# End of a segment in layer A: order of the last values, scores and output rounds, and a second home for an attention output

## The chip, the cores and the metric

The kernel runs on one core of a Trainium2 chip. Its metric is the device time of one execution in microseconds (us), as the median of several runs. Engines: TensorE (PE in the profile, its weight loads PEld), VectorE (DVE), ScalarE (ACT), GpSimd (POOL) and SyncE (SP). Each engine works through its own queue in order and waits for the others by semaphores. DMA transfers are issued here from SP's queue (weights) and from POOL's queue (small rows).

## The reference, cut to what matters

Four layers, A B A B, each added to the residual. Layer A, the one that the change touches, walks through the 2048 tokens in 64 segments of 32 tokens. Eight memory rows come ahead of each segment; they are the first eight output rows of the segment before, so segments can't be computed side by side.

```
for s in range(n_seg):                       # 64 segments
    h = concat([mem, x[32 s : 32 s + 32]])   # 40 rows of 640
    q, k, v = h @ Wq, h @ Wk, h @ Wv         # 32 heads of 192
    p = softmax(mask(q k^T * scale))         # 40 x 40 per head
    o = (p v) @ Wo                           # 40 rows of 640
    mem = o[:8]; out = o[8:]
```

Layer B is a linear attention with a learned feature map over all tokens. It is not changed.

## The kernel before, in words

`layer_A` first runs `A_pre`, which computes K, Q and V of the last eight tokens of every segment for all segments at once and stores them in DRAM (`kqb`, `vb`). `A_chain` then walks through the 64 segments, and this serial walk is most of the kernel's time. All bf16 weights of a layer A don't fit on the chip with the rest, so part of Wq, Wk and Wv goes through slots that SP loads again in every segment (`load_slot`, L661), and the twelve chunks of Wo for the first and last round share one region, `wo_end`, loaded again in every segment in six parts (`load_wo`, L678).

The 32 heads are worked in four rounds n = 0..3 of eight heads, in the order 0,1,2,3 in even segments and 3,2,1,0 in odd ones. For one round:

- `project` (L957) multiplies the transposed rows `hT` with the weights of one matrix: 5 steps of 4 matmuls, each into its own 32 rows of one PSUM bank (ps_qk for Q and K, ps_v for V). Where a piece of the weights lies in a slot, the matmul needs that slot's DMA.
- `to_raw` (ScalarE, L980) copies Q or K out of PSUM, `to_rows` (VectorE, L985) transposes it into QT or KT. `v_rows` (L994) copies V into one of two Vp tiles, one half on ScalarE, one on VectorE. KT has 80 columns for each of six row blocks: 64 from the transpose, 16 that POOL copies from kqb (`extra_kq`, L946). Rows 64 to 80 of Vp come by DMA from `vb` (`extra_v`, L953, the "V tail").
- `scores` (L1005): a matmul that writes the mask, then 6 with KT and QT, into ps_s. `weigh` (L1063) adds the exponential on ScalarE, giving E; for the last round E lies in the buffer of tag "raw".
- `sums` (L1079): a matmul with ones gives the softmax's sums. `normalise` (L1083): logarithm and exponential on ScalarE, a multiplication on VectorE (L1087).
- `attend` (L1018): 8 matmuls of Vp and E into two banks ps_o; ScalarE and VectorE copy one half each into OT (L1027, L1028). `keep_tail` and `store_tail` keep the 16 columns of the last eight tokens and store them by a POOL DMA. `tails_after` issues the V tail for two rounds later, and `next_kq` (L1071) copies the next round's extra keys and queries and loads the `kqb` after next.
- `wo_round` (L1043): 12 steps of 4 matmuls that add OT times Wo into ps_w, one bank for the whole segment.

Nothing plans this order: `tc.manual_schedule()` leaves the instructions of every engine as they are written, and only the waits are put in. A round's parts are written one round apart, so that an attention, which needs finished weights E, stands behind the next round's projections. The loop `for n in range(L)` (L1133, L = 3) writes, for n = 0, 1, 2: Q of round n+1, attention n-1, scores n, K of round n+1, sums and normalisation n, output round n-1, V of round n+1 (not for n = 2). The end of the segment (from L1159) writes: scores 3, three fifths of V of round 3, attention 2, sums 3, the rest of V, output round 2, four filler matmuls (`keep_busy`, L1052, results unused), attention 3, five fillers, output round 3, five fillers, and `fill` (L1058), weight loads of one column. Then VectorE transposes the memory rows out of ps_w into the next `hT`, and the next segment's Q can begin. The attentions and rounds are named here by their place 0 to 3 in the segment; "second output round" in the change's title means the round with index 1.

Of the kernel before, what the change touches and what calls it, by code (L numbers as in the profile page):

```python
# [8 lines left out]
P = 128  # L9
BF16 = mybir.dt.bfloat16  # L10
# [8 lines left out]
LN_EPS = 1e-5  # L19

FILL = {0: 86, 2: 78}
SEG_FILL = 1

LATE = 64512
ARENA = 202752
# [90 lines left out]
class Kernel:  # L116
# [784 lines left out]
    def A_chain(self, xn_dram, at_dram, li, load_slot, piece, load_wo, late_wo, wo_mid, wo_end, low):  # L901
# [3 lines left out]
        with tc.tile_pool(name=f"A{li}_ch", reuse_waits="tile", bufs=1) as sp, \  # L905
# [3 lines left out]
            KT = sp.tile([P, 6, 80], BF16, name="KT")  # L909
# [105 lines left out]
                                         start=False, stop=(x == 1 and i == 2), skip_group_check=True)  # L1015
                return S

            def attend(E, n):  # L1018
                O = [pop.tile([P, 512], F32, name=f"ps_o{x}", tag=f"o{x}") for x in range(2)]
                for x in range(2):  # L1020
                    for k, e, i in ((0, 0, 0), (320, 1, 2), (128, 0, 1), (192, 1, 1)):
                        nc.tensor.matmul(O[x][:, 80 * i:80 * i + 80], lhsT=Vs[n % 2][0:80, 448 * x + k:448 * x + k + 128],  # L1022
                                         rhs=E[0:80, 160 * x + 80 * e:160 * x + 80 * e + 80], start=(k == 0),
                                         stop=(k == 192), skip_group_check=True)
                OT = sp.tile([P, 6, 64], BF16, name="OT", tag="OT")
                o = [x[:, 0:240].rearrange("p (i q) -> p i q", q=80) for x in O]
                nc.scalar.activation(out=OT[:, 0:3, :], in_=o[0][:, :, 0:64], func=ACT.Copy)  # L1027
                nc.vector.tensor_copy(out=OT[:, 3:6, :], in_=o[1][:, :, 0:64])  # L1028
                return OT, o

# [9 lines left out]
            def store_tail(otb, s, r):  # L1040
                nc.gpsimd.dma_start(out=self.otb_d[s, :, 96 * r:96 * r + 96], in_=otb[:, :, :].rearrange("p c t -> p (c t)"))  # L1041

            def wo_round(W, r, OT, first, last):  # L1043
                w = wo_end[:, :] if r in (0, 3) else wo_mid[:, 7680 * (r - 1):7680 * r]
                for i in range(12):
                    c, q = i % 6, 32 * (i // 6)
                    for g in range(4):
                        nc.tensor.matmul(W[32 * g:32 * g + 32, 0:160], lhsT=OT[:, c, q:q + 32],  # L1048
                                         rhs=w[:, 640 * i + 160 * g:640 * i + 160 * g + 160], start=(first and i == 0),
                                         stop=(last and i == 11), tile_position=(0, 32 * g), skip_group_check=True)  # L1050
# [51 lines left out]
            for s in range(NSEG):  # L1102
                W = pop.tile([P, 512], F32, name="ps_w", tag="w")
                order = rounds(s)
                L = NR - 1

                def q_or_k(m, n):
                    ps = pqp.tile([P, 512], F32, name="ps_qk", tag="qk")
                    project(hT, ps, m, n, s, range(KC))
                    return to_raw(ps, "OT" if m == "K" and n == 0 else "raw")  # L1110

                def v_banks():
                    return pop.tile([P, 512], F32, name="ps_v", tag="v")

                def tails_after(n):
                    if n + 2 < NR:
                        extra_v(s, n + 2)
                    elif s + 1 < NSEG:
                        extra_v(s + 1, n + 2 - NR)

                to_rows(q_or_k("Q", 0), "Q")
                if s == 0:
                    fill(FILL[li])
                to_rows(q_or_k("K", 0), "K")
                if s == 0:
                    late_wo(2)
                if s > 0:
                    store_rows(s - 1)
                pv = v_banks()
                project(hT, pv, "V", 0, s, range(KC))  # L1130
                v_rows(pv, 0)
                Ep = None
                for n in range(L):  # L1133
                    raw = q_or_k("Q", n + 1)
                    if n > 0:
                        OT, o = attend(Ep, n - 1)
                        tails_after(n - 1)
                    S, E = weigh(False)
                    to_rows(raw, "Q")
                    if n > 0:  # L1140
                        otb = keep_tail(o)
                    next_kq(s, n)
                    if n > 0:
                        store_tail(otb, s, order[n - 1])
                    to_rows(q_or_k("K", n + 1), "K")
                    sums(S, E)
                    normalise(S, E)
                    if n > 0:
                        wo_round(W, order[n - 1], OT, n == 1, False)
                        if n == 1:  # L1150
                            load_wo(order[L])
                            if s == NSEG - 1:
                                load_wo(3, low[:, 0:7680])
                    if n + 1 < L:
                        pv = v_banks()
                        project(hT, pv, "V", n + 1, s, range(KC))
                        v_rows(pv, n + 1)
                    Ep = E
                S, E = weigh(True)  # L1159
                pv = v_banks()  # L1160
                project(hT, pv, "V", L, s, range(3))
                OT, o = attend(Ep, L - 1)
                tails_after(L - 1)
                otb = keep_tail(o, True)
                next_kq(s, L)
                store_tail(otb, s, order[L - 1])
                sums(S, E)
                project(hT, pv, "V", L, s, range(3, KC))
                v_rows(pv, L, "x")
                normalise(S, E)  # L1170
                v_rows(pv, L, "a")
                if s + 1 < NSEG:
                    hT = new_hT()
                    hx_transpose(hT, range(1))
                wo_round(W, order[L - 1], OT, False, False)
                idle = pqp.tile([P, 512], F32, name="ps_idle", tag="qk")
                keep_busy(idle, 4, 192)
                OT, o = attend(E, L)
                tails_after(L)
                if s + 1 < NSEG:  # L1180
                    hx_transpose(hT, range(1, 4))
                    if s + 2 < NSEG:
                        load_rows(s + 2)
                keep_busy(idle, 5, 230)
                wo_round(W, order[L], OT, False, True)
                keep_busy(idle, 5, 230)
                fill(SEG_FILL)
                if s + 1 < NSEG:
                    wt = sp.tile([P, KC, 32], F32, name="wt", tag="raw")
                    for b0, b1 in ((2, 5), (0, 2)):  # L1190
                        nc.vector.transpose(out=wt[:, b0:b1, :], in_=W[:, 0:160].rearrange("p (j b) -> p b j", b=KC)[:, b0:b1, :])  # L1191
                        nc.vector.tensor_copy(out=hT[:, b0:b1, 0:8], in_=wt[:, b0:b1, 0:8])  # L1192
                store_tail(keep_tail(o), s, order[L])
                keep_rows(W)
# [73 lines left out]
```

## Time and profile before

| What | us |
|---|---|
| median of 3 runs (3625.7 to 3645.58) | 3634.94 |
| the profiled execution's own time | 3630.61 |
| its span, first to last instruction | 3628.6 |
| first layer A's chain, first to last counted segment | 206.5 to 1521.7 |
| second layer A's chain, likewise | 2027.0 to 3347.3 |

| Engine | busy us | share of the span |
|---|---|---|
| PE | 3489.8 | 96% |
| PEld | 2274.3 | 63% |
| DVE | 2329.9 | 64% |
| ACT | 2040.9 | 56% |
| POOL | 1591.3 | 44% |

How to read it: the shares are means over the whole kernel, and matmul ends are modelled, so a busy PE isn't a PE at its peak. The DMA engines moved 933.33 MB, a mean of 257 GB/s. A chain-of-waits line gives a start, a length and what ran. A row of the timeline gives start, length, engine, line, operation, names and shapes, and in brackets the idle time before it and what ended it. A row of the waits gives who waited for whom, the total in us, how often, and the longest. A row of DMA issues gives the KB of each and the median us from issue to landing.

### The profile page before, as it was taken

Reading aid. Unit: us, or ns where it says so; the run is one execution under the profiler, and the core shown is the slowest. Engines: PE = TensorE matmul, PEld = TensorE weight load, DVE = VectorE, ACT = ScalarE, POOL = GpSimd, SP = SyncE. Lnnn points to the kernel's source line nnn. Section 1 sums busy time; section 2 is a strip of 40 time slices with the busy share of each in tenths; the row PEclk is TensorE's granted clock in tenths of the full one; section 3 lists DMA queues with packets and bytes.
Section 4 is the critical chain, followed back from the end, with each engine's and each line's share of the span. In section 5 each row is a group of like instructions: output and inputs, shape, how many; then the busy total and the mean of one; then the engine's idle time right before and its main releaser. Section 6 shows DMA issues by size and latency. Waiting matters only on the chain.

```text
span 3628.6 us, 168597 instructions
## 1 busy us (share of the span) xinstructions
PE 3489.8 (96%) x70944; PEld 2274.3 (63%) x71270; DVE 2329.9 (64%) x6336; ACT 2040.9 (56%) x5233; POOL 1591.3 (44%) x4181
## 2 busy tenths in 40 slices
PE   9989999999999999989999899999999999999899
PEld 7756666666666666655377566666666666666553
DVE  5557666666666667646643566766666666667465
ACT  3356666666666666546432555666666666666463
POOL 3445555555555545430123454555545555555300
PEclk9999999999999999999999999999999999999999
DMA  8988887887888878860387877888888888888700
GB/s 295 339 292 292 283 290 277 292 293 276 290 294 282 281 279 296 289 202 1 138 271 203 304 271 268 292 288 286 279 292 284 280 283 288 295 275 291 230 1 30
DMA packets 533266, 933.33 MB, mean 257 GB/s; under 512 B 141066, under 2 KB 300442, under 8 KB 532506
## 3 DMA queue, kind: packets, MB, share of 16 engines
q1 hardware_dynamic: 431098, 821.50, 64.2%
q0 software_dynamic: 67744, 87.80, 8.3%
q10 hardware_dynamic: 33664, 13.24, 1.4%
q8 instruction: 557, 9.13, 1.0%
q14 instruction: 203, 1.66, 0.1%
HBM read 852.43 MB, written 73.73 MB: 255 GB/s over the span
## 4 chain that ended last, share of the span: by engine, by line
PE 68%; DMA 9%; DVE 8%; issue 6%; ACT 6%; PEld 2%; POOL 2%; SPq 0%; POOLq 0%; DVEq 0%; ACTq 0%
PE ps_qk L972 20%; PE ps_w L1048 8%; PE ps_v L972 8%; PE ps_o L1022 5%; PE ps_s L1014 4%; PE ps_pre L863 4%; DMA arena<-wo_rows 4%; DVE hT L928 3%; PE ps_s L1080 3%; PE ps_s L1009 2%; PE ps_pre L887 2%; PE ps_idle L1055 2%; DMA Vp<-vb 2%; ACT raw L982 2%; DVE E L1087 2%
## 5 line engine op out<-in xcount | busy, mean ns | idle before, releaser
L972 PEld LDWEIGHTS <-hT 128*32 128x32 bf16 x30720 | 738.8, 96 | 434.6 <-DVE hT L1192 29.5
L972 PE MATMUL ps_qk<-arena,hT 128*32 128x384 bf16 x20480 | 997.1, 327 | 13.1 <-DMA arena<-in_A_Wk_dram 3.1
L982 ACT ACTIVATE raw<-ps_qk 128x384 bf16<-128x384 f32 x1024 | 502.0, 490 | 381.1 <-PE ps_s L1080 245.7
L1048 PE MATMUL ps_w<-arena,OT 128*32 128x160 bf16 x24576 | 537.6, 235 | 25.9 <-issue 15.6
L955 POOL DMA_DIRECT2D Vp<-vb x512 | 258.3, 505 | 656.0 <-PE ps_o L1022 448.6
L972 PE MATMUL ps_v<-arena,hT 128*32 128x384 bf16 x10240 | 536.5, 329 | 6.0 <-DMA arena<-in_A_Wv_dram 6.0
L1048 PEld LDWEIGHTS <-OT 128*32 128x32 bf16 x24576 | 435.0, 97 | 114.7 <-issue 37.5
L987 DVE STREAM_TRANSPOSE KT<-raw 128x384 bf16<-128x384 bf16 x512 | 296.0, 578 | 196.5 <-ACT raw L982 192.5
L990 DVE STREAM_TRANSPOSE QT<-raw 128x256 bf16<-128x256 bf16 x512 | 227.9, 445 | 237.7 <-ACT raw L982 195.9
L943 POOL DMA_DIRECT2D kqb<-kqb x512 | 290.9, 568 | 173.6 <-POOL KT L951 147.6
L1003 DVE CAST Vp<-ps_v 64x384 bf16<-64x384 f32 x512 | 286.2, 559 | 95.7 <-ACT Vp L1001 80.8
L1001 ACT ACTIVATE Vp<-ps_v 64x384 bf16<-64x384 f32 x512 | 246.1, 481 | 151.0 <-PE ps_v L972 113.7
L1041 POOL DMA_DIRECT2D otb<-otb x512 | 282.8, 552 | 109.4 <-DVE otb L1037 94.5
L1028 DVE CAST OT<-ps_o 128x192 bf16<-128x192 f32 x512 | 182.9, 357 | 214.6 <-PE ps_o L1022 196.7
L1087 DVE TENSOR_TENSOR E<-E,ps_s 80x320 bf16<-80x320 bf16 x512 | 247.5, 483 | 73.6 <-ACT ps_s L1086 69.6
L1066 ACT ACTIVATE E<-ps_s 80x320 bf16<-80x320 f32 x512 | 221.4, 432 | 122.9 <-PE ps_s L1014 94.8
L1022 PEld LDWEIGHTS <-Vp 80*128 80x128 bf16 x4096 | 183.1, 99 | 160.3 <-issue 122.8
L1022 PE MATMUL ps_o<-E,Vp 80*128 80x80 bf16 x4096 | 234.0, 202 | 24.5 <-DMA Vp<-vb 4.5
L1014 PE MATMUL ps_s<-QT,KT 128*80 128x80 bf16 (+1 forms) x3072 | 233.2, 213 | 22.2 <-DVE KT L987 13.8
L1027 ACT ACTIVATE OT<-ps_o 128x192 bf16<-128x192 f32 x512 | 167.7, 328 | 147.7 <-PE ps_o L1022 147.7
L936 ACT ACTIVATE Vp<-ps_w 32x160 bf16<-32x160 f32 x512 | 150.3, 294 | 171.3 <-DVE wt L1191 146.1
L1014 PEld LDWEIGHTS <-KT 128*80 128x80 bf16 x3072 | 194.7, 119 | 70.6 <-issue 60.9
(151 smaller groups left out, 5213.8 us busy)
## 6 DMA issues: line engine op xcount, KB each, us to landing
arena<-wo_rows SPq DMA_DIRECT2D x792, 320.0 KB, 6.8
arena<-in_A_Wq_dram SPq DMA_DIRECT2D x427, 384.0 KB, 4.6
arena<-in_A_Wv_dram SPq DMA_DIRECT2D x427, 384.0 KB, 6.4
arena<-in_A_Wk_dram SPq DMA_DIRECT2D x768, 192.0 KB, 4.6
kqb<-kqb POOLq DMA_DIRECT2D x512, 48.0 KB, 5.1
arena<-in_A_Wk_dram SPq DMA_DIRECT2D x43, 384.0 KB, 7.0
vb<-arena POOLq DMA_DIRECT2D x128, 112.0 KB, 6.0
Vp<-vb POOLq DMA_DIRECT2D x512, 28.0 KB, 4.9
```

The source lines that it names most:

```text
L943: nc.gpsimd.dma_start(out=kqb[:], in_=self.kqb_d[s, :, r, :])
L955: nc.gpsimd.dma_start(out=Vs[n % 2][64:80, :], in_=self.vb_d[s, r].rearrange("g t f -> (g t) f"))
L972: nc.tensor.matmul(o[32 * g:32 * g + 32, 0:384], lhsT=hT[:, b, :], rhs=rhs, start=(i == 0), stop=(i == KC - 1), tile_position=(0, 32 * g), ...
L982: nc.scalar.activation(out=raw[:], in_=ps[:, 0:384], func=ACT.Copy)
L987: nc.vector.transpose(out=KT[:, :, 0:64], in_=raw[:, :].rearrange("p (c j) -> p c j", j=64))
L1001: nc.scalar.activation(out=o, in_=i, func=ACT.Copy)
L1003: nc.vector.tensor_copy(out=o, in_=i)
L1014: nc.tensor.matmul(S[0:80, c0:c0 + 80 * (q1 - q0)], lhsT=KT[:, 3 * x + i, :], rhs=QT[:, x, q0:q1, :], start=False, stop=(x == 1 and i == 2 ...
L1022: nc.tensor.matmul(O[x][:, 80 * i:80 * i + 80], lhsT=Vs[n % 2][0:80, 448 * x + k:448 * x + k + 128], rhs=E[0:80, 160 * x + 80 * e:160 * x ...
L1041: nc.gpsimd.dma_start(out=self.otb_d[s, :, 96 * r:96 * r + 96], in_=otb[:, :, :].rearrange("p c t -> p (c t)"))
L1048: nc.tensor.matmul(W[32 * g:32 * g + 32, 0:160], lhsT=OT[:, c, q:q + 32], rhs=w[:, 640 * i + 160 * g:640 * i + 160 * g + 160], start=(firs ...
L1087: nc.vector.tensor_tensor(out=E[0:80, 0:320], in0=E[0:80, 0:320], in1=rc, op=ALU.mult)
```

## The change

The diff reorders the end of a segment and changes three details.

- V of round 3 is written whole directly behind the loop, ahead of the last scores, and both halves are copied out there.
- The output round of index 1 leaves the loop's last turn (n = 2). It is written in four parts instead: steps 0 to 3 ahead of the scores, 4 and 5 behind them, 6 and 7 behind attention 2, 8 to 11 behind the sums. `wo_round` gets an argument `part` for it.
- The output of attention 1 has to live through all four parts, so attention 2 writes its output to another place: the first 64 columns of KT's six blocks, which the last scores have read by then. `attend` gets an argument `OT` for it.
- The four fillers ahead of attention 3 get 96 columns instead of 192, and `SEG_FILL` is 2 instead of 1: one weight load more at the segment's end.

```diff
--- before.py
+++ after.py
@@ -19,7 +19,7 @@
 LN_EPS = 1e-5
 
 FILL = {0: 86, 2: 78}
-SEG_FILL = 1
+SEG_FILL = 2
 
 LATE = 64512
 ARENA = 202752
@@ -1015,14 +1015,15 @@
                                          start=False, stop=(x == 1 and i == 2), skip_group_check=True)
                 return S
 
-            def attend(E, n):
+            def attend(E, n, OT=None):
                 O = [pop.tile([P, 512], F32, name=f"ps_o{x}", tag=f"o{x}") for x in range(2)]
                 for x in range(2):
                     for k, e, i in ((0, 0, 0), (320, 1, 2), (128, 0, 1), (192, 1, 1)):
                         nc.tensor.matmul(O[x][:, 80 * i:80 * i + 80], lhsT=Vs[n % 2][0:80, 448 * x + k:448 * x + k + 128],
                                          rhs=E[0:80, 160 * x + 80 * e:160 * x + 80 * e + 80], start=(k == 0),
                                          stop=(k == 192), skip_group_check=True)
-                OT = sp.tile([P, 6, 64], BF16, name="OT", tag="OT")
+                if OT is None:
+                    OT = sp.tile([P, 6, 64], BF16, name="OT", tag="OT")
                 o = [x[:, 0:240].rearrange("p (i q) -> p i q", q=80) for x in O]
                 nc.scalar.activation(out=OT[:, 0:3, :], in_=o[0][:, :, 0:64], func=ACT.Copy)
                 nc.vector.tensor_copy(out=OT[:, 3:6, :], in_=o[1][:, :, 0:64])
@@ -1040,9 +1041,9 @@
             def store_tail(otb, s, r):
                 nc.gpsimd.dma_start(out=self.otb_d[s, :, 96 * r:96 * r + 96], in_=otb[:, :, :].rearrange("p c t -> p (c t)"))
 
-            def wo_round(W, r, OT, first, last):
+            def wo_round(W, r, OT, first, last, part=range(12)):
                 w = wo_end[:, :] if r in (0, 3) else wo_mid[:, 7680 * (r - 1):7680 * r]
-                for i in range(12):
+                for i in part:
                     c, q = i % 6, 32 * (i // 6)
                     for g in range(4):
                         nc.tensor.matmul(W[32 * g:32 * g + 32, 0:160], lhsT=OT[:, c, q:q + 32],
@@ -1145,8 +1146,8 @@
                     to_rows(q_or_k("K", n + 1), "K")
                     sums(S, E)
                     normalise(S, E)
-                    if n > 0:
-                        wo_round(W, order[n - 1], OT, n == 1, False)
+                    if n == 1:
+                        wo_round(W, order[n - 1], OT, True, False)
                         if n == 1:
                             load_wo(order[L])
                             if s == NSEG - 1:
@@ -1156,25 +1157,28 @@
                         project(hT, pv, "V", n + 1, s, range(KC))
                         v_rows(pv, n + 1)
                     Ep = E
+                pv = v_banks()
+                project(hT, pv, "V", L, s, range(KC))
+                v_rows(pv, L)
+                OT1 = OT
+                wo_round(W, order[L - 2], OT1, False, False, range(4))
                 S, E = weigh(True)
-                pv = v_banks()
-                project(hT, pv, "V", L, s, range(3))
-                OT, o = attend(Ep, L - 1)
+                wo_round(W, order[L - 2], OT1, False, False, range(4, 6))
+                OT, o = attend(Ep, L - 1, KT[:, :, 0:64])
                 tails_after(L - 1)
                 otb = keep_tail(o, True)
                 next_kq(s, L)
                 store_tail(otb, s, order[L - 1])
+                wo_round(W, order[L - 2], OT1, False, False, range(6, 8))
                 sums(S, E)
-                project(hT, pv, "V", L, s, range(3, KC))
-                v_rows(pv, L, "x")
+                wo_round(W, order[L - 2], OT1, False, False, range(8, 12))
                 normalise(S, E)
-                v_rows(pv, L, "a")
                 if s + 1 < NSEG:
                     hT = new_hT()
                     hx_transpose(hT, range(1))
                 wo_round(W, order[L - 1], OT, False, False)
                 idle = pqp.tile([P, 512], F32, name="ps_idle", tag="qk")
-                keep_busy(idle, 4, 192)
+                keep_busy(idle, 4, 96)
                 OT, o = attend(E, L)
                 tails_after(L)
                 if s + 1 < NSEG:
```

## The prediction

> **What bounds the kernel now.** I read the chain that ended last first, then one segment of layer A in order of time, then the waits, then the landings of transfers.
>
> ```profile
> PE 68%; DMA 9%; DVE 8%; issue 6%; ACT 6%; PEld 2%; POOL 2%; SPq 0%; POOLq 0%; DVEq 0%; ACTq 0%
> ```
>
> TensorE's order of work sets the time, with transfers second. The two layers A hold 128 segments. Counting from a segment's first Q matmul to the next one's, the commonest period is 20.91 us, and 62 periods in the first layer (206.5 to 1521.7 us) average 21.21, those in the second (2027.0 to 3347.3) 21.30. So 0.35 us a segment are irregular waits. The segment from 1223.42 to 1244.33 has the common period. This is its chain from the end of round 2's sums to round 3's output (start us, us, what):
>
> ```profile
> 1237.19 0.94 PE ps_w L1048 x48
> 1238.13 0.26 PE ps_s L1009
> 1238.39 0.05 issue
> 1238.44 0.45 PE ps_s L1014 x6
> 1238.90 0.60 PE ps_v L972 x12
> 1239.50 0.39 PE ps_o L1022 x8
> 1239.89 0.14 PE ps_s L1080
> 1240.03 0.44 PE ps_v L972 x8
> 1240.47 0.85 PE ps_w L1048 x48
> 1241.32 0.44 PE ps_idle L1055 x4
> 1241.76 0.01 issue
> 1241.77 0.45 PE ps_o L1022 x8
> ```
>
> The reader is to see that TensorE hardly waits in these 4.58 us, and that the third attention (1241.77) follows 0.44 us of filler matmuls. The filler covers the chain from the last sums (end 1240.03) over logarithm, exponential and multiplication. The multiplication (L1087, 1241.14 to 1241.62) and ScalarE's half of the V copy (L1001, also 1241.14 to 1241.62) end last.
>
> The transfers that meet this stretch:
>
> ```profile
> Vp<-vb POOLq DMA_DIRECT2D x1, 28.0 KB, 5.8
> arena<-wo_rows SPq DMA_DIRECT2D x1, 320.0 KB, 7.6
> ```
>
> The first is the tail rows of the third attention's V, issued at 1235.87 (L955). It lands at 1241.65, 0.12 before that attention. The second is the sixth and last part of the output weights for the closing round, issued at 1235.7. It lands at 1243.3, while that round (1242.71 to 1243.70) is already running. From 1228 to 1240 the sixteen DMA engines show a share of 1.01 to 1.07, so these landings are set by a full queue. The waits of TensorE in the whole trace:
>
> ```profile
> PE ps_w L1048 <- issue: 15.6, 29, 1.5
> PE ps_w L1048 <- DMA arena<-wo_rows: 9.4, 14, 3.3
> PE ps_o L1022 <- DMA Vp<-vb: 4.5, 8, 1.5
> ```
>
> Both transfers already stop TensorE now and then. The "issue" row is always the same matmul, the sixth or so of the second attention's output round, and it starts about 1.45 us after the third of the segment's four 16 KB instruction blocks has arrived.
>
> **The change, part by part: TensorE's order.** The same stretch from 1237.19, in the new order.
> - V of round 3 comes whole: 20 matmuls, 0.81 us as in the segment's other rounds, where the halves now cost 0.60 + 0.44. Gain 0.23.
> - Second output round, first third: 0.31. The mask matmul: 0.26. So the scores start at 1238.57, and K's transpose (L987) ends at 1238.30: the wait is gone and they take 0.29 as in the other rounds, not 0.05 + 0.45. Gain 0.21. End 1238.86.
> - A sixth of the round (0.16), the second attention (0.39) from 1239.02, just behind its weights E (ready 1238.96). A sixth (0.16), the sums (0.14) to 1239.71, a third (0.31) to 1240.02. The four parts cost the 0.94 of the round; I take nothing for starting four times.
> - Next output round 0.85, filler halved: 0.22 instead of 0.44. Gain 0.22. The filler's cover is the softmax chain: the sums end 0.32 earlier, and now VectorE is free, so the multiplication ends 0.04 + 0.41 + 0.03 + 0.41 + 0.02 + 0.48 = 1.39 after them, at 1241.10; both are ready near 1241.15.
>
> So TensorE alone could begin the third attention 0.60 earlier: 77 us in 128 segments. Behind 1241.77 nothing is removed.
>
> **What lies beside.** V's copies (ScalarE 0.48, VectorE 0.56) move ahead. ScalarE copies 1238.47 to 1238.95, so the last exponential starts at 1238.97 instead of 1238.93; done at 1239.40, the sums need it at 1239.57. VectorE's half ends at 1239.55, when the second attention's copies are due anyway. These copies into KT follow the scores in TensorE's order, so no new wait. The one weight load more (0.08) sits behind the closing filler, before a 0.2 us idle. On POOL's queue the V tail for the next segment, four copies, one kqb load and one otb store keep their order and come about 0.5 earlier with the second attention; in the full queue they could delay the last weights by under 0.1. No DMA of SP moves. A new wait is possible: V of round 3 now needs its third streamed weight slot at about 1237.85, and it lands at 1237.7. Over all segments I find it late in 13%, 0.05 us on average, with the whole of TensorE's queue behind it; the next wall hides that.
>
> **The walls.** I read every landing (the sixteenth update of its semaphore) in 124 segment periods, relative to the segment's first matmul. The V tail lands at 18.10 (median; one in ten below 17.93 or above 18.56), the last weights at 19.86 (19.24 to 20.26). Both issues hang on work before the changed stretch, so they stay. The third attention begins at 18.345 undisturbed, and the period is the later of attention start + 2.56 and last weights + 0.96. That rule gives a mean of 21.24 where 21.25 is measured. With the change the attention starts at the latest of 17.75, tail + 0.06, and instruction block + 2.40 (2.62 now; the 0.22 of filler). The mean over the same 124 segments becomes 21.07. The tail sets almost all starts, the last weights 48 of the ends. **Sum:** 0.167 x 128 = 21 us, an estimate from these landings; 56 of the 77 go into the two transfers. Without the tail's wall it would be 36, without the weights' 32, without the instruction block's 28.
>
> **Two rules weighed.** The Trainium skill, "DMA: Bandwidth & Descriptors", section "Anatomy of one DMA — SWDGE (gpsimd) path", fits 2.0 us plus bytes/436e3 for a transfer from POOL's queue. That makes 2.07 us for these 28 KB: the tail would be there at 1237.9, and the gain 36 us. The row says 5.8 in this stage (1.8 is the shortest of the trace). I take the row, so 21. "TensorE: Matmul & The Clock Gate", section "Why this matters for your kernels", wants no idle gap above some 3 us, else half clock. By that the shorter filler and the new waits, under 1 us each, cost nothing. The trace is stricter: after the waits of 1.94 and 1.97 us in two segments the granted clock fell to half for one 3.41 us window (windows 46 and 58% idle), and each of these periods lost 0.4 to 1.4 us beyond the wait; windows up to 40% idle, and one of 48%, kept it. The change makes typical ends some 30% idle, so I expect a handful more of such windows, about 5 us at most, and leave it to the range.
>
> **Rivals.**
> - *More of the gain survives.* If tail and weights land 0.3 earlier than I read, because the copies and stores of POOL lie otherwise between them, the gain is about 45, up to the 77. For it: the landings are one execution's. Against: both follow from what is issued before the change. Time 3590.
> - *Nothing arrives.* If they land 0.2 later (the next segment's 100 KB of POOL's queue now overlap the weights), the rule gives 0. For it: the queue is full until 1240. Against: only 28 KB of the 100 move into that stretch. Time 3635.
> - *Slower.* One mechanism: the second attention's output now shares KT with POOL's copy of the next round's extra keys (L951, now 1241.40 to 1241.66, then near 1241.2). If the output round has to wait for that copy, it starts at 1241.2 instead of 1240.02, the third attention at about 1242.4, 0.65 later than now, and the rule gives 54 us more: 3688. It decides as soon as that wait passes 0.6 us. Against it: where a tile is shared already, POOL does not wait for VectorE's other columns, the two overlap:
>
> ```profile
> 1236.11 0.45 DVE L990 STREAM_TRANSPOSE QT<-raw 128x256 bf16<-128x256 bf16 x1
> 1236.37 0.25 POOL L948 COPY QT<-kqb 128x64 bf16<-128x64 bf16 x1
> ```
>
> The half clock is a smaller way to the same side: 0.9 us each, it would need 40 of the 128 ends to cost 18 us on balance.
>
> **How the numbers follow.** The profiled execution took 3630.6 us (span 3628.6 and 2.0 around it). Less 21 it is 3609.6; the median of the runs is 4.3 higher, which gives 3614. Walls as read: 0.48, with its own range 3600 to 3626. More survives: 0.17. Nothing: 0.15. Slower: 0.20, KT and half clock together. A change below 0.5% (18 us) is about what a measurement of this kernel can't tell from none: faster means below 3617. Of the first case some two thirds lie there, with the second 0.51; the rest of the first and the third make 0.29; slower 0.20. The range, 3572 to 3656, takes in the gain of up to 63 and the start of the slower case, and leaves out most of that case and a little of the second.
>
> **What would show it.** Right: TensorE's V x20 directly before a split output round; no wait at the scores; an idle stretch of about 0.4 us ahead of the third attention, ended by the V tail; more and longer waits of L1048 for wo_rows; a common period near 20.7 to 21.0. Wrong: a third attention 0.6 earlier with no such waits, a wait of the output round for POOL L951, or many half-clock windows inside the layers.

## The result

The changed kernel takes 3630.11 us (median of 20 runs, 3615.61 to 3645.47), the kernel before in the same measurement 3641.85 us (20 runs, 3625.7 to 3650.57). The ratio is 0.9972, with a 95% interval of 0.9959 to 0.9986: some 10 us gained (12 between the medians), where 21 were forecast. Single executions of one kernel differ by more than that: the two profiled ones that stand side by side, 3630.6 before and 3628.7 after, are 2 us apart.

The line of the chain that ended last, after:

```profile
PE 57%; DMA 19%; DVE 7%; issue 7%; ACT 5%; POOL 3%; PEld 2%; SPq 0%; POOLq 0%; DVEq 0%; ACTq 0%
```

DMA has 19% of it instead of 9%, TensorE 57% instead of 68% (in a second profile of each kernel, DMA 17% after and 13% before). The waits of TensorE in the whole trace say which transfers:

```profile
PE ps_v L972 <- DMA arena<-in_A_Wv_dram: 15.1, 18, 3.6
PE ps_w L1049 <- DMA arena<-wo_rows: 15.0, 25, 4.2
PE ps_w L1049 <- issue: 11.7, 30, 0.9
PE ps_o L1022 <- DMA Vp<-vb: 10.9, 28, 1.1
```

The wait of attention 3 for the V tail went from 4.5 to 10.9 us and from 8 to 28 times (5.4 to 9.1 in the second profiles). That for the last output weights went from 9.4 to 15.0 us here, but from 15.8 to 12.0 in the second profiles, so no growth is shown for it. The stalls that the profile calls "issue" shrank, from 15.6 to 11.7 and from 20.6 to 10.8 us. The first row is new in this length (6.0 us, 4 times before): V waits for the streamed slots of Wv. Some 9 of its 15.1 us lie in the first segments of the two layers A, treated below.

Undisturbed segments show what the new order itself does. This is the chain of one, which starts at 3152.56 (start us, us, what), over the stretch that the forecast worked out:

```profile
3166.07 0.26 PE ps_s L1081
3166.33 0.93 PE ps_v L972 x20
3167.26 0.28 PE ps_w L1049 x16
3167.53 0.26 PE ps_s L1009
3167.79 0.29 PE ps_s L1014 x6
3168.08 0.25 PE ps_w L1049 x8
3168.34 0.39 PE ps_o L1022 x8
3168.73 0.25 PE ps_w L1049 x8
3168.98 0.26 PE ps_s L1081
3169.24 1.22 PE ps_w L1049 x64
3170.46 0.28 PE ps_idle L1056 x4
3170.74 0.42 PE ps_o L1022 x8
```

The reader is to see that nothing waits here, and that the stretch is longer than forecast all the same. From the end of round 2's sums (3166.33) to the filler (3170.46) TensorE works 4.13 us; the forecast had 0.81 + 0.31 + 0.26 + 0.29 + 0.16 + 0.39 + 0.16 + 0.14 + 1.16 = 3.68, and the kernel before takes 4.13 as well (1237.19 to 1241.32). **TensorE saves nothing at all in this stretch.** The starts that the trace records, as medians over the 30 shortest periods of each profile, in us from the segment's first Q matmul:

| | before | after |
|---|---|---|
| end of the loop: first matmul behind round 2's sums | 13.70 | 13.70 |
| sums of round 3 | 16.30 | 16.35 |
| filler | 17.81 | 17.84 |
| attention 3 | 18.35 | 18.13 to 18.18 |
| best periods | 20.91 | 20.69 |

Still 0.2 us are gained, all of it between filler and attention. The sums don't come earlier, but what follows them is shorter: the copies of V no longer stand among logarithm, exponential and multiplication. Before, the multiplication waited for VectorE's half of V and attention 3 for ScalarE's half, which ended together with it, 1.59 us after the end of the sums; now the multiplication ends 1.40 after that end (3169.24 to 3170.64).

The transfers that land on this stretch of that segment (issue rows: queue, count, KB, us to landing):

```profile
arena<-wo_rows SPq DMA_DIRECT2D x1, 320.0 KB, 7.4
Vp<-vb POOLq DMA_DIRECT2D x1, 28.0 KB, 5.4
```

The V tail takes 5.4 us and lands 0.3 ahead of the attention here. Over all 124 counted periods it lands at 18.16 after the segment's start (median; 18.11 before), and the last weights at 19.90 (19.86 before). The landings stayed where they were.

### The profile page after: what moved, and what is told of

It reads as the page before. It is cut to its first block, busy times and chain, and to the rows that moved or that the text cites. A ratio compares the mean times of both kernels' runs of the same rounds, so it can differ in the third digit from the quotient of the medians.

```text
span 3627.0 us, 168472 instructions
## 1 busy us (share of the span) xinstructions
PE 3484.6 (96%) x70944; PEld 2279.2 (63%) x71398; DVE 2332.7 (64%) x6336; ACT 2040.4 (56%) x5233; POOL 1598.2 (44%) x4181
## 4 chain that ended last, share of the span: by engine, by line
PE 57%; DMA 19%; DVE 7%; issue 7%; ACT 5%; POOL 3%; PEld 2%; SPq 0%; POOLq 0%; DVEq 0%; ACTq 0%
PE ps_qk L972 17%; DMA arena<-wo_rows 7%; PE ps_w L1049 7%; PE ps_v L972 6%; DMA Vp<-vb 5%; PE ps_o L1022 4%; PE ps_pre L863 3%; DMA arena<-in_A_Wv_dram 3%; PE ps_s L1014 3%; DVE hT L928 2%; PE ps_s L1081 2%; PE ps_s L1009 2%; PE ps_pre L887 2%; PE ps_wo L410 2%; PE ps_idle L1056 1%
## 5 line engine op out<-in xcount | busy, mean ns | idle before, releaser
L972 PEld LDWEIGHTS <-hT 128*32 128x32 bf16 x30720 | 753.5, 96 | 453.5 <-issue 29.5
L972 PE MATMUL ps_v<-arena,hT 128*32 128x384 bf16 x10240 | 515.6, 328 | 15.7 <-DMA arena<-in_A_Wv_dram 15.1
L1049 PE MATMUL ps_w<-arena,OT 128*32 128x160 bf16 x18432 | 471.3, 235 | 16.0 <-DMA arena<-wo_rows 15.0
L1049 PEld LDWEIGHTS <-OT 128*32 128x32 bf16 x18432 | 321.1, 96 | 116.5 <-issue 23.6
L1022 PE MATMUL ps_o<-E,Vp 80*128 80x80 bf16 x4096 | 235.6, 203 | 26.3 <-DMA Vp<-vb 10.9
L1086 ACT ACTIVATE ps_s<-ps_s 80x320 f32<-80x320 f32 x512 | 215.3, 420 | 41.6 <-PE ps_s L1081 41.6
L948 POOL COPY QT<-kqb 128x64 bf16<-128x64 bf16 x512 | 125.4, 245 | 252.6 <-PE ps_s L1014 244.7
```

Source lines behind the costliest of these rows:

```text
L972: nc.tensor.matmul(o[32 * g:32 * g + 32, 0:384], lhsT=hT[:, b, :], rhs=rhs, start=(i == 0), stop=(i == KC - 1), tile_position=(0, 32 * g), ...
```

## The experiments

**Theory A**: what the split order saves on TensorE it spends again at each change between two kinds of matmuls. V, Q, K and the output round write four column groups of 32 rows (`tile_position`); mask, scores, attention, sums and fillers use the array as a whole. Each change, in either direction, costs some 0.1 us. The recorded starts show it without the modelled ends (medians over the 30 shortest periods): 48 output matmuls take 0.84 us up to V's first matmul and 0.94 up to a mask or a filler; where the attention follows the scores, it starts 0.30 after them (`light_vfirst`, below), eight output matmuls 0.39 after them. Between round 2's sums and the filler there are six changes before and eight after. What in the change costs the time, the tile position or the other shapes of weights that come with it, no run separates. **Theory B** is the forecast's: the attention could start 0.60 earlier, and the transfers hide most of it. **Theory C**: it is the choice of executions, and nothing is gained but spread. The period and the chain below are those of the 124 counted segment periods in the two layers A.

**The kernels once more, for the spread of one execution.** First the kernel before:

> The kernel before once more, unchanged, for a second profile. It asks whether the landings that I took as fixed walls are the same in another execution. In the changed kernel's profile the third instruction block arrived at 15.65 us after the segment's start (median) instead of 15.33, the last output weights at 19.90 on average instead of 19.81. If the change moved them, this profile shows again 15.3 and 19.8. If executions differ by themselves, it shows other values, up to 0.3 away, and a mean period up to 0.1 us (13 us in all) away from 21.25.

One run of 3652.36 us. Its profile has a mean period of 21.36 us, where the profile that the forecast read has 21.25. The last weights land at 20.03 on average instead of 19.81, the third instruction block at 15.74 (median) instead of 15.33, and the "issue" wait of the output round comes 49 times instead of 29. The best periods are the same, 20.90. So the execution behind the forecast was one with early landings. The kernel after:

> The changed kernel once more, unchanged, for a second profile. Theory of the switches and walls: attention 3 again never before 18.13 us after the segment's start, the same four waits (V tail, last weights, instruction block, third V slot) in front of TensorE with some 35 to 45 us in all; the first segments of the two layers take 76 us together, where the kernel before took 70 and 73. If the first profile's first segments (38.4 and 38.1) were chance, they are 70 to 73 here too.

One run of 3628.91 us, mean period 21.15 (21.23 in the first profile); attention 3 starts at 18.09 at the earliest. The mean of two profiles each: the chain of the 124 periods takes 2642.1 us before and 2627.8 after, 14.4 less. The first segments of the two layers together take 71.7 before and 76.4 after, 4.7 more. That makes 9.7 less, near the measured gain. How near is in part luck: the two chains of one kernel lie 13 us apart before and 10 after, and the rest of the program varies by some 10 us between executions.

**Without the last round's output weights.** In four kernels the line that loads them again is gone, old weights are used, and 1.97 MB a segment less is moved (`light_two` and `again_light_after`, below, are of this kind too):

```diff
                         if n == 1:
-                            load_wo(order[L])
                             if s == NSEG - 1:
```

That removes the last weights' wall, and with the queue emptier the tail's and the instruction block's too. First the kernel before in this form:

> The kernel before without the reload of the output weights for the segment's last round: that round uses old weights, and a third of the transfers of a segment (1.97 MB) is gone. With it all walls should go. Expected by every theory: nearly every period at 20.91 us, no wait of TensorE for V tail, wo_rows or instruction blocks, total 35 to 43 us below the kernel before.

Ratio 0.9877 (0.9859 to 0.9895), mean period 21.00, commonest 20.91. TensorE's waits for the V tail and for "issue" are gone. Then the kernel after:

> The changed kernel with the same left out. Theory of the forecast (TensorE's order is worth 0.60 us a segment, the walls took most of it): period 20.31 us, 77 us below the light kernel before. Theory of the switches (each change between column-tiled and whole-array matmuls costs TensorE about 0.1 us, and the split round has more of them): period 20.69 to 20.70, 27 us below the light kernel before. Theory that the order is worth nothing: no difference.

Ratio 0.9862 (0.9838 to 0.9886), mean period 20.85, commonest 20.69. With these three walls out of the way the change is worth 0.22 us in an undisturbed period and 0.15 on average (0.21 with the second profile of this kernel, `again_light_after`), not 0.60. That is against Theory B. The slots of Wv are still waited for, 6.3 us in the 124 periods, so they are a wall of their own. In the total little is seen, since the first segments take 79.5 us instead of 69.0.

With three parts instead of four, in the same form:

```diff
                 S, E = weigh(True)
-                wo_round(W, order[L - 2], OT1, False, False, range(4, 6))
                 OT, o = attend(Ep, L - 1, KT[:, :, 0:64])
...
-                wo_round(W, order[L - 2], OT1, False, False, range(6, 8))
+                wo_round(W, order[L - 2], OT1, False, False, range(4, 8))
```

> The light changed kernel with the second output round in three parts instead of four: steps 4 and 5 are written with 6 and 7 behind the second attention, so scores and attention, both whole-array, follow each other. Theory of the switches: 0.1 us a segment less TensorE time, 12 us below the light changed kernel, as far as the softmax chain, ready at the same time now, moves with it. Theory of the forecast (a part costs its matmuls alone): no difference within 2 us.

Ratio 0.9843 (0.9818 to 0.9868), no different from the four parts. Attention 2 starts at 15.60 instead of 15.71, which looks like the 0.1 us that was expected, but isn't. Eight matmuls and two changes no longer stand ahead of it; at 0.30 us behind the scores' start (15.07) it could begin at 15.37. It has to wait for its weights E, whose multiplication ends at 15.54 with four and with three parts. So most of what the missing changes save is lost to that wait, and the eight matmuls now come behind it: the sums still start at 16.36 and attention 3 at 18.14. This run says little for or against Theory A.

V whole and ahead of the scores in the kernel before, again without these loads, the output round left in one piece:

```diff
-                S, E = weigh(True)
                 pv = v_banks()
-                project(hT, pv, "V", L, s, range(3))
+                project(hT, pv, "V", L, s, range(KC))
+                v_rows(pv, L)
+                S, E = weigh(True)
                 OT, o = attend(Ep, L - 1)
```

> The light kernel before (no reload of the last round's output weights), with V of round 3 written whole ahead of the last scores and nothing else of the change: output round 1 stays whole in front, filler 192. Theory of the switches: TensorE saves 0.11 on V (one start less) and 0.21 at the scores, the sums end at about 1240.2 on the clock of the segment shown, and the softmax chain of 1.40 us behind them sets attention 3 at 18.2 to 18.25 instead of 18.345: period 20.78 to 20.80. Theory of the forecast (parts cost their matmuls alone): the sums end 0.1 earlier, period 20.70.

One run of 3628.85 us; commonest period 20.90, mean 21.24. Its chain at the scores (start us, us, what):

```profile
581.23 0.30 PE ps_s L1014 x6
581.53 0.02 issue
581.55 0.44 ACT E L1066
582.00 0.04 issue
582.04 0.30 PE ps_s L1080
```

This miss taught something: with only the attention between scores and sums, the sums wait for ScalarE's exponential (0.23 us in each of 124 periods), and the gain is gone. The many other stalls of this profile, 37 times "issue" for 23 us in the 124 periods and all over the segment, belong to the finding on instruction blocks below: this kernel, too, has 1023 TensorE instructions in a segment.

**Without the V tail of round 3.** In the kernel after, the transfer is left out in all segments but a layer's first:

```diff
                     if n + 2 < NR:
-                        extra_v(s, n + 2)
+                        if n != 1 or s == 0:
+                            extra_v(s, n + 2)
```

> The changed kernel without the DMA of V's tail rows for the last round of a segment (28 KB; the attention uses an old tail). Theory of the walls: the wait of attention 3 for the tail (11 us in the changed kernel) goes, the third instruction block and the last weights stop TensorE instead in part, mean period 21.10, some 12 us below the changed kernel, ratio to the kernel before near 0.994. Rival, that the last weights alone set the end: less than 4 us. Rival, that the tail alone hides the forecast's gain: attention 3 comes down to 17.75 in undisturbed segments instead of 18.13.

Ratio 0.9913 (0.9892 to 0.9934), mean period 21.02, attention 3 at a median of 18.18 and never before 18.10, so the tail doesn't hide a start at 17.75. Leaving the tail out is worth some 21 us to the kernel after, so the transfers do hold gain back; that the queue has 28 KB less to move is part of it. The forecast's own figure for this wall was 15 (36 against 21).

**The old order in the first segment.** There all streamed weights of the layer arrive for the first time, and late.

```diff
-                    if n == 1:
-                        wo_round(W, order[n - 1], OT, True, False)
+                    if n == 1 or (s == 0 and n == 2):
+                        wo_round(W, order[n - 1], OT, n == 1, False)
...
+                if s == 0:
+                    S, E = weigh(True)
+                    pv = v_banks()
+                    project(hT, pv, "V", L, s, range(3))
+                    OT, o = attend(Ep, L - 1)
...
+                else:
```

> The changed kernel with the old order in the first segment of each layer alone. Theory that the first segments lose because V of round 3 now stands ahead of work that needs no late weights: the two first segments take 70 to 73 us instead of 76, the total is 4 us below the changed kernel, ratio to the kernel before 0.996. Rival, that the first segments end with their last transfer whatever the order: 76 us, ratio 0.997.

Ratio 0.9975 (0.9959 to 0.9991); the two first segments take 73.8 us. In the kernel after, V stands there where it stops everything behind it (first of three such rows of the timeline; in brackets the idle time and what ended it):

```profile
195.71 0.35 PE L972 MATMUL ps_v<-arena,hT 128*32 128x384 bf16 x4 [3.42 <-DMA arena<-in_A_Wv_dram]
```

The other two waits are 0.85 and 0.68 us. In the kernel before there are two, of 2.45 and 0.61 us, behind the output round; with the old order put back they are 0.87 and 0.61 (2.11 and 0.86 in the second layer). Half of the 4.7 us comes back, less than expected, and it isn't seen in the total.

**The V tail on another queue.** ScalarE's queue sends it for the fourth round:

```diff
-                nc.gpsimd.dma_start(out=Vs[n % 2][64:80, :], in_=...)
+                (nc.scalar if n == 3 else nc.gpsimd).dma_start(out=Vs[n % 2][64:80, :], in_=...)
```

> The kernel after, with one edit: the tail rows of V for the fourth round are sent by ScalarE's own DMA queue instead of POOL's. All work stays. Theory (the tail's landing holds the third attention; with its transfer left out the chain's 124 periods fell from about 21.19 to 21.02 us): if the other queue brings the 28 KB in 2 to 4 us instead of 5.8, waits of the attention for the tail go from some 32 per profile to under 10, mean period 21.05 to 21.10, ratio to before 0.992 to 0.994. Rival (the sixteen engines are full, whichever queue asks): landing at about 18.1 after the segment's start as now, 30 waits, ratio 0.997. Second rival: the early landing only uncovers the last output weights and the third V slot, then the waits change names and the ratio is 0.995 to 0.997.

Ratio 0.997 (0.9955 to 0.9984), no different from the kernel after. Its waits of TensorE:

```profile
PE ps_w L1049 <- issue: 19.4, 38, 1.3
PE ps_w L1049 <- DMA arena<-wo_rows: 18.4, 34, 4.0
PE ps_v L972 <- DMA arena<-in_A_Wv_dram: 16.1, 24, 4.8
PE ps_s L1081 <- ACT E L1067: 4.2, 11, 0.6
PE ps_o L1022 <- DMA Vp<-vb: 0.5, 2, 0.3
```

The tail lands at 17.80 instead of 18.16 and is hardly waited for. Of these 0.36 us, 0.26 are the earlier issue (12.19 instead of 12.45); on the way it is hardly faster. The other three rows have grown by about what was saved, and there is a fourth: issuing the transfer takes ScalarE's queue 0.31 us. SP issues the last weights at 13.17 instead of 11.98. The second rival was right: the waits change names.

**The filler.** At its old length of 192 columns:

```diff
-                keep_busy(idle, 4, 96)
+                keep_busy(idle, 4, 192)
```

> The kernel after with the filler matmuls ahead of the third attention at their old length, 192 columns instead of 96 (0.44 instead of 0.22 us, about 0.28 as shown in the kernel after). Theory: what the change leaves of its 0.60 us is only this filler, because the new changes of tiling between the four parts cost what the V and the scores save; then the third attention starts at 18.34 to 18.36 undisturbed, the commonest period is 20.89 to 20.92, and the ratio to before is 1.000 (0.998 to 1.003, the first segments of the layers 5 us longer, the waits for the landings shorter). Rival (the forecast's working, without its filler: 0.38 saved): attention at 17.97, commonest period 20.69 or less, ratio 0.997 as in the kernel after.

Ratio 0.9999 (0.9983 to 1.0016), best period 20.73, attention 3 at 18.20 by its recorded start in the shortest 30 periods. The ratio is what was expected, but not for the reason given, since neither of the two periods came. An undisturbed segment, from 912.93 to 933.67 (chain):

```profile
930.84 0.44 PE ps_idle L1056 x4
931.27 0.30 PE ps_o L1022 x8
```

The chain's ends are modelled: it puts the filler's end at 18.34 after the segment's start, and leaves the attention 0.30 instead of 0.42. The recorded start of the attention is 18.20, and the period of 20.74 agrees with that one. So undisturbed the shorter filler is worth 0.04 to 0.06 us, and some 0.15 of the 0.2 are the softmax without V's copies. The filler did become shorter by more than that: with 192 columns the attention starts 0.36 us after it, with 96 as little as 0.18 (`light_two`, below). But with four parts the weights E, ready at 18.08, hold the attention at 18.13. Where TensorE itself is late (behind "issue" or a slot), the whole filler is on the path, 0.16 us; by the rule of the forecast that makes 3 us in all, an estimate. The measured difference to the kernel after is 10 with some 8 of uncertainty, and what else is in it stays open.

**The one weight load at the segment's end.**

```diff
-SEG_FILL = 2
+SEG_FILL = 1
```

> The kernel after with the last filler of a segment at 1 as before, not 2: one weight load less on TensorE, 0.08 us in front of an idle time, and 1023 instead of 1024 TensorE instructions in a segment. Theory (instruction blocks arrive at the same place of each segment only because a segment is a whole number of blocks of 256): the place of the stall drifts by one instruction a segment through the whole segment, and stalls called issue move to many lines; some of these places have less work in hand, ratio to before 0.999 to 1.006. Rival (the one load more means nothing): 0.997, stalls at the sixth matmul of the second attention's output round as before.

3734.64 us, ratio 1.0204 (1.0168 to 1.024). The largest effect of all edits that keep the kernel's work, from 0.08 us of it taken away. The waits of TensorE:

```profile
PE ps_w L1049 <- issue: 66.8, 68, 2.4
PE ps_o L1022 <- issue: 22.1, 15, 2.4
PE ps_idle L1056 <- issue: 17.4, 17, 2.0
```

A segment has exactly 1024 TensorE instructions before and after (matmuls, weight loads, waits for semaphores), four blocks of 256. In each segment four transfers of 16 KB run on the queue that the profile calls "instruction", and each stall ends about 1.4 us after one of them has landed. The change removes one separate wait instruction, that of attention 3 for two semaphores, and the second weight load makes up for it. With 1023 the place where a block begins moves by one instruction a segment, and the stalls move through the segment, with 111 of them and 111 us in the 124 periods instead of 30 and 12. In the 124 periods twelve stretches of half the granted clock follow, where the kernel after has one. With 1024 the stalls lie at one place, the 797th instruction of the segment (all 30 after, 29 of 31 before). That other places have less work in hand is the likely reason for the longer stalls; no run tests it.

**Two parts instead of four**, as a version that might beat both. Counted in single changes it has four where the four parts have eight:

```diff
-                wo_round(W, order[L - 2], OT1, False, False, range(4))
+                wo_round(W, order[L - 2], OT1, False, False, range(6))
                 S, E = weigh(True)
-                wo_round(W, order[L - 2], OT1, False, False, range(4, 6))
                 OT, o = attend(Ep, L - 1, KT[:, :, 0:64])
...
-                wo_round(W, order[L - 2], OT1, False, False, range(6, 8))
                 sums(S, E)
-                wo_round(W, order[L - 2], OT1, False, False, range(8, 12))
+                wo_round(W, order[L - 2], OT1, False, False, range(6, 12))
```

> The kernel after with the second output round in two parts instead of four, all work kept: 24 matmuls ahead of the last scores, then mask, scores, second attention and sums together, then the other 24. Theory (each change between matmuls in four column groups and matmuls over the whole array costs some 0.10 us, and the third attention follows the softmax of the last sums): two changes fewer, sums starting at 16.05 to 16.20 after the segment's start instead of 16.35, filler reached at 17.60 to 17.65 instead of 17.84, third attention undisturbed at 17.95 to 18.05 instead of 18.13, best period 20.55 to 20.60 instead of 20.69. Of that little is left behind the tail's landing (median 18.16): more waits of the attention for the tail, 40 to 60 instead of 32, ratio to before 0.9955 to 0.9965. Rival (the sums have to wait for the exponential of the last scores, as they did where nothing lay between): third attention at 18.13 or later, ratio 0.997 to 0.999.

Ratio 0.9979 (0.996 to 0.9997): no better. Its best period is 20.52, its mean 21.33. The waits:

```profile
PE ps_v L972 <- DMA arena<-in_A_Wv_dram: 27.0, 42, 4.0
PE ps_w L1049 <- DMA arena<-wo_rows: 21.0, 43, 3.2
PE ps_w L1049 <- issue: 16.6, 32, 1.1
PE ps_s L1081 <- ACT E L1067: 13.0, 57, 0.2
```

The waits grew at the slots of Wv and the last weights, not at the tail as expected, and the sums now wait for the exponential. To see whether the order or the transfers had failed, the same order without the last round's output weights, and beside it the four parts in this form again:

> The output round in two parts, and without the last round's output weights being loaded again in the later segments (old ones are used, 1.97 MB a segment less). Theory (two parts do shorten TensorE's order, and with the full queue the transfers took that back): best and commonest period 20.52 to 20.56 instead of 20.69, mean period 20.72 to 20.78, 8 to 16 us below the four parts without these loads. Rival (the wait of the sums for the exponential is worth what the two changes save): commonest period 20.68 to 20.70, no difference.

> The kernel after without the last round's output weights being loaded again, a second time, as the comparison for the two parts: commonest period 20.69, mean period 20.85, ratio 0.986 as before.

3556.46 us against 3586.19: ratios 0.9791 (0.9776 to 0.9806) and 0.9878 (0.986 to 0.9897). Commonest periods 20.52 and 20.69, mean 20.62 and 20.79; the chain of the 124 periods differs by 21 us, more than the 8 to 16 expected. The stretch with two parts (the segment starts at 2632.20):

```profile
2645.98 0.93 PE ps_v L972 x20
2646.90 0.41 PE ps_w L1049 x24
2647.32 0.26 PE ps_s L1009
2647.58 0.30 PE ps_s L1014 x6
2647.88 0.02 issue
2647.91 0.44 ACT E L1067
2648.35 0.04 issue
2648.39 0.30 PE ps_s L1081
2648.69 1.36 PE ps_w L1049 x72
2650.05 0.28 PE ps_idle L1056 x4
2650.32 0.30 PE ps_o L1022 x8
```

By recorded starts the sums begin at 16.18 instead of 16.35 and attention 3 at 17.95 instead of 18.13, though the sums wait 0.14 for the exponential and attention 2, at 15.60, for its E. So fewer changes do shorten the segment, by 0.17 us, and with all transfers running this is lost to other waits.

## Why the prediction was right or wrong

- **The mechanism** was right in kind: the attention starts earlier, the V tail stops it more often, and part of what the order allows is lost to landings. That these bind is shown by leaving them out (0.9913 without the tail). The sizes were wrong. The order allows 0.22 us a period, not 0.60, and so the transfers take far less of it than forecast: in the 124 periods 14.4 us arrive, where 19 to 26 do without the last weights' loads (0.15 to 0.21 a period).
- **"The four parts cost the 0.94 of the round; I take nothing for starting four times"** is the step that failed. Eight output matmuls take 0.25 instead of 0.16, twice. The sums take 0.26 instead of 0.14, since they now follow output matmuls and no longer the attention. V, "0.81 as in the segment's other rounds", takes 0.93, since it follows the sums. Together with w x64 (1.22 for 1.16) and x16 (0.28 for 0.31) that is 0.45, and it uses up the 0.23 of V and the 0.21 of the scores. Counted in single changes, the new order has two more, which cost 0.2, as much as the end of the scores' wait gives back. The 0.23 claimed for V never existed: the halves' 0.60 + 0.44 contain two changes that the new order still has, at other places. It could have been read from the kernel before (chain; V stands behind an output round, the mask behind the attention, K behind the scores):

```profile
1000.41 0.81 PE ps_v L972 x20
1002.04 0.39 PE ps_o L1022 x8
1002.43 0.14 PE ps_s L1009
1002.57 0.29 PE ps_s L1014 x6
1002.86 0.93 PE ps_qk L972 x20
1003.79 0.26 PE ps_s L1080
```

Twenty matmuls of V or K take 0.81 behind column groups and 0.93 behind whole-array work, the sums 0.26 behind K and, in the forecast's own lines, 0.14 behind the attention.
- **The scores' wait** is gone (0.29 directly behind the mask), as forecast.
- **The filler**: 0.22 were claimed, undisturbed it is 0.04 to 0.06. The softmax chain after the sums was forecast at 1.39 and takes 1.40, but the sums themselves were to come 0.32 earlier and come 0.05 later. So the weights E hold the attention until 18.13, not 17.75.
- **"So they stay"**, of the landings: right, within 0.1 us. But their level came from one execution, with early ones. The same kind of rule with 18.13 for 17.75 gives 0.11 us a period on those landings and 0.09 on the other profile's (14 and 11 us in 124 periods, an estimate); measured on two profiles each are 14.4. With 17.75 kept, it gives 0.10 on the second profile's landings, and worked out again on the first ones 0.13, where the forecast has 0.167. So of the 11 us that are missing, some 6 lie in the 124 periods (0.167 a period would be 20.7), and 4.7 in the first segments. How the 6 divide between the starting point, the one execution and the rule itself stays open.
- **The third V slot**: late in 13% of segments and 0.05 us on average was forecast; it is some 16 of 124 and 6 us (15 and 5 in the second profile), so about 13% and 0.05. What was missed is the first segment of each layer, where the new order costs 4.7 us in all.
- **The weight load more** was put at nothing, and costs nothing that shows (best period 20.69 with it, 20.70 without). That it is needed was not seen: without it the kernel after is 2% slower than the kernel before.
- **The slower rival** didn't happen. VectorE's copy into KT and POOL's copy of the extra keys stand apart, and the output round never waits for POOL:

```profile
3168.77 0.36 DVE L1029 CAST KT<-ps_o 128x192 bf16<-128x192 f32 x1
3170.24 0.26 POOL L951 COPY KT<-kqb 128x96 bf16<-128x96 bf16 x1
```

The round that reads KT's new columns starts at 3169.46, 0.78 before POOL writes its own. Half clock didn't happen either: inside the counted periods there are two such windows before and one after.
- **More survives** (3590) fell with the 0.60; **nothing arrives** (3635) is the nearest of the times named; the gain of 10 to 12 us lies midway between its 0 and the forecast's 21. The size, 0.28%, is below the 0.5% that the forecast took as measurable; only because both kernels ran 20 times does the interval exclude 1.
- **The rule on POOL's transfers** (the Trainium skill, "DMA: Bandwidth & Descriptors", "Anatomy of one DMA — SWDGE (gpsimd) path") was set aside for the row, rightly: 5.4 us here. The runs show where the rule holds: without the output weights in the queue the same tail takes 2.1 to 2.4 us (issue 12.45, landing at 14.62 to 14.87, medians of three kernels), near the 2.07 of the page.

## What to carry to other kernels

Before splitting a run of matmuls, look for the same matmul in the profile behind its new predecessor: here each change between column-group and whole-array matmuls costs 0.1 us, and four parts cost all that the reordering saved. When a step comes earlier in a test, look at what held it, too: it may be the next wait and not the step that was changed. A wall made of landings should be read from more than one execution. Here the same tail on another queue moved the waits to other transfers, and only bytes left out removed them. Look at the count of an engine's instructions per loop turn before changing it; here a whole number of instruction blocks kept the stalls in one place.

## What the runs showed that was not expected

- One TensorE instruction less in a segment (1023 for 1024) costs 2.3% against the same kernel with it (1.0204 against 0.997 of the kernel before): 111 us of stalls for instruction blocks in the 124 periods instead of 12.
- In the layers A the DMA engines move 284 to 286 GB/s before and after alike, and 284 and 282 with two parts. With 1.97 MB a segment less they move 195 to 201 GB/s, the tail lands 3.3 us earlier, the third instruction block about 2 us earlier, and no stall for a block is left at that place. Three kinds of waits (tail, last weights, blocks) had one cause, the output weights' loading in that stretch. The waits for the slots of Wv did not go with it.
- Taking V's copies out from among the steps of the softmax is what gained most of the undisturbed 0.2 us, though TensorE's own order became no shorter: the multiplication ends 1.40 instead of 1.59 us after the sums.
